# A gated linear recurrence and a gated feed-forward on one core: the order lists behind the first sums laid out anew

## The chip, the cores and the metric

The kernel runs on one core of a Trainium2 chip. Its measure is the device time of one execution in microseconds (us), lower is better. The kernel before took 194.64 us, the median of three runs (194.61, 194.64, 195.2).

## What is computed

Two operations follow each other. The first is a recurrence over 768 time steps for 4 batches of 8 heads with 48 dimensions, the second a feed-forward over the 3072 rows that come out of it.

```python
def _attn_ref(q, k, v, f_logit):
    f = 1.0 / (1.0 + np.exp(-f_logit))
    state = np.zeros((B, H, D, D))
    for t in range(S):
        state = f[:, :, t, :, None] * state + np.einsum('bhd,bhe->bhde', k[:, :, t], v[:, :, t])
        y[:, :, t] = np.einsum('bhd,bhde->bhe', q[:, :, t], state)
    return y

x = attn_out.transpose(0, 2, 1, 3).reshape(B * S, H * D)       # 3072 x 384
gate = np.maximum(x @ w_gate, 0.0)                              # 384 x 1536
val = x @ w_val
return gate * val @ w_out                                       # 1536 x 384
```

## The kernel before, in words

Time is cut into 6 chunks of 128 steps. The work is told by (chunk c, position b), four positions to a chunk; the first eight such pieces are done two at a time as a "unit" (two chunks of one batch), the others one batch each. For every piece the kernel sums -log f along time with a matmul (`cum`), takes exponentials of the sums (`ek`, `eq`), scales k and q by them (`hk`, `hq`, the tile `hats`), transposes these (on TensorE as `tk`, `tq` with copies `ck`, `cq` into `qkT` for the first eight pieces, with a DMA, `xh`, for the others), forms scores (`s`), masks them (`m`, into `ptm`), and multiplies by v (`y`, and `yi` for what comes from the state). `kv` is the chunk's contribution to the state, `ss`, `sd` and `st` (VectorE or GpSimd) bring the state forward. The result goes, transposed, into `xT` (`x`, or `n` and a DMA `xx`).

The feed-forward of a chunk has 12 slices of 128 hidden columns: a gate group `g` and a value group `u` (three matmuls each), relu `r`, product `p` into `gT`, and then per position three output groups `o` of four matmuls, a copy `d` and a store `S`. In chunk 0 the first four slices are done in two halves of 256 columns (`g00.j`, `g02.j`), the others over 512.

An operation's name is the short name with chunk and position: `hk10` is k scaled for chunk 1, position 0; `g00.8` is gate slice 8 of chunk 0; `o03.4` the second output group of chunk 0, position 3. Loads of inputs are named `f1.2`, `k1.0` and so on (384 KB each, for two positions); those of the weights `wg4+4` (gate slices 4 to 7), `wv0+2`, `wo8+4`. Weights are converted to bf16 by the transfer and are issued by GpSimd's queue (POOL), inputs by SP and ScalarE (ACT), stores by SP.

The program decides no order by itself. Each operation is an `Op` with a number, with one or more engines that can do it, and with what it reads and writes. `Plan.link` (line 127) derives the dependences. The lists in `ORDER` (line 23) give for every engine the numbers in the order of issue, and by standing in a list an operation is put on that engine. `BANKS` gives each accumulator its PSUM bank, in the order of TensorE's list. A negative entry `~3512` in TensorE's list means three filler matmuls of 512 columns on zeros (line 877); ahead of them TensorE already waits for whatever holds the next operation's bank. `HELD` adds waits by hand: `51: 53` makes operation 51 (`wg0+2`) wait until 53 (`k0.2`) has landed; as lists are issued in order, what stands behind 51 in its queue waits too. `Plan.waits` (line 187) turns dependences into semaphore waits.

Numbers that come up: 66 `q1.2`, 59 `k1.0`, 60 `q1.0`, 65 `k1.2`, 64 `f1.2`, 61 `v1.0`, 67 `v1.2`, 70 `wo0+2`, 52 `wv0+2`, 51 `wg0+2`, 57 `wv2+2`, 62 `wg4+4`, 63 `wv4+4`, 69 `wv8+4`, 68 `wg8+4`, 71 to 73 the other `wo`; 117 and 127 `hq02`, `hq03`; 116 and 126 `hk02`, `hk03`; 236 and 246 `hk10`, `hk11`; 273 `hq12`; 102 `y00`; 266 `ef12` (exponential of f, line 478); 159 `r00.3`; 150 `g00.1`; 289 `s12`; 302 `g10.0`; 806 `q5.2`; 928 and 929 the copy and store of the last piece's 256 columns, 933 and 934 of its 128.

Of the kernel before, what the change touches and what calls it, by code (L numbers as in the profile page):

```python
# [21 lines left out]

ORDER = {
    "PE": [
        45, ~60100, 76, 87, ~4512, 84, ~3512, 92, 82, 103, ~2512, 94, ~1512, 112, 123, 97, ~2512, 120, ~2512, 130, ~3512,
        118, ~3512, 102, 106, 139, 128, ~3512, 158, 133, 232, 154, 243, 150, 152, ~1512, 146, 156, 160, 138, 142, 268, 279,
# [13 lines left out]
    ],  # L40
    "ACT": [
# [8 lines left out]
    ],  # L50
    "DVE": [
# [12 lines left out]
    ],  # L64
    "POOL": [
# [4 lines left out]
    ],  # L70
# [5 lines left out]
    ],  # L76
}

HELD = {
    51: 53, 59: 62, 61: 71, 63: 58, 65: 63, 66: 57, 70: 55, 71: 60,  # L80
}

BANKS = [
# [9 lines left out]
]  # L93


# [847 lines left out]
```

## Time and profile before

| what | value |
|---|---|
| median of the runs | 194.64 us |
| the profiled execution | 195.66 us, span 193.8 us |
| TensorE (PE) busy | 187.2 us, 97% |
| of it fillers of 512 columns | 24 matmuls; 60 more of 100 columns ahead of the first data |
| VectorE (DVE) busy | 141.4 us, 73% |
| ScalarE (ACT) / GpSimd (POOL) busy | 89.1 us / 53.1 us |
| transfers | 32.44 MB, 110311 packets |
| first filler-free stretch, `g00.0` | starts at 23.48 us |
| chunk 1's first gate group, `g10.0` | starts at 55.39 us |

The profiled execution is 1.0 us longer than the median of the runs; times within the profile are counted from the start of the span. A row of the timeline gives start, duration, engine, line and operation, out<-in, the number of instructions, and in brackets the idle time before it with what ended it. In the queues' rows stand packets, MB and the time that the packets took as a share of 16 engines; q0 is the queue of the weights, q1 SP's, q10 ScalarE's.

### The profile page before, as it was taken

What the parts mean: (1) busy time and instruction counts of PE and PEld (TensorE: products, weight loads), DVE (VectorE), ACT (ScalarE), POOL (GpSimd) and SP (SyncE); (2) the same over time, 40 slices, a digit from 0 to 9 for tenths busy, and PEclk for the clock granted to TensorE, in tenths of its full rate; (3) what the DMA queues carried; (4) which work ended last, traced back from release to release, by engine and by line L of the source; (5) the groups of instructions that cost most, each with busy time, mean ns of one, the idle gap of its engine ahead of it and who ended that gap; (6) DMA issues with size and microseconds to landing.
All of it is one profiled execution on the core that took longest, in us unless ns stands there. A gap on an engine that the chain in (4) does not pass through costs nothing.

```text
span 193.8 us, 4881 instructions
## 1 busy us (share of the span) xinstructions
PE 187.2 (97%) x2009; PEld 109.5 (57%) x2009; DVE 141.4 (73%) x264; ACT 89.1 (46%) x191; POOL 53.1 (27%) x84
## 2 busy tenths in 40 slices
PE   7899999999899999999999999999999999999994
PEld 7555676565554555655546755656555565555554
DVE  4486957896946899988998878988649585373331
ACT  2776962340189931274624895663241313424300
POOL 8867500920338204134011415227100000000000
PEclk9999999999999999999999999999999999999999
DMA  5999999999998999999999988757670022002113
GB/s 148 325 284 211 139 192 260 215 195 263 244 221 176 251 199 192 192 239 190 255 215 184 218 238 171 155 145 148 139 191 3 20 81 64 16 26 81 41 43 123
DMA packets 110311, 32.44 MB, mean 167 GB/s; under 512 B 103504, under 2 KB 110032, under 8 KB 110288
## 3 DMA queue, kind: packets, MB, share of 16 engines
q1 hardware_dynamic: 93056, 25.04, 58.5%
q0 software_dynamic: 3776, 3.54, 11.6%
q10 hardware_dynamic: 13456, 3.54, 8.2%
q8 instruction: 16, 0.26, 0.5%
q14 instruction: 7, 0.06, 0.1%
HBM read 25.95 MB, written 4.72 MB: 158 GB/s over the span
## 4 chain that ended last, share of the span: by engine, by line
PE 70%; DMA 19%; ACT 4%; POOL 4%; issue 1%; ACTq 0%; DVE 0%; POOLq 0%; DVEq 0%
PE ps L792 39%; PE ps L813 20%; DMA k_in<-in_k_dram 9%; DMA v_in<-in_v_dram 5%; DMA wg<-in_moe_w_gate_dram 3%; POOL hats L540 3%; DMA wo<-in_moe_w_out_dram 2%; PE ps L584 2%; PE ps L503 1%; PE ps L745 1%; PE ps L772 1%; ACT expo L516 1%; PE ps L756 1%; ACT bneg L481 1%; ACT expo L518 1%
## 5 line engine op out<-in xcount | busy, mean ns | idle before, releaser
L800 DVE TENSOR_TENSOR gT<-relu,ps 128x512 bf16<-128x512 bf16 (+1 forms) x76 | 48.6, 655 | 22.1 <-PE ps L792 16.2
L792 PE MATMUL ps<-xT,wv 128*128 128x512 bf16 (+1 forms) x228 | 58.0, 368 | 0.2 <-issue 0.2
L792 PE MATMUL ps<-xT,wg 128*128 128x512 bf16 (+1 forms) x228 | 57.8, 368 | 0.2 <-ACT xT L597 0.2
L813 PE MATMUL ps<-wo,gT 128*128 128x384 bf16 (+2 forms) x300 | 51.9, 320 | 0.3 <-DMA wo<-in_moe_w_out_dram 0.3
L797 ACT ACTIVATE relu<-ps 128x512 bf16<-128x512 f32 (+1 forms) x47 | 27.2, 584 | 39.8 <-PE ps L792 19.8
L813 PEld LDWEIGHTS ps<-wo,gT 128*128 128x128 bf16 x300 | 27.6, 98 | 19.0 <-DMA wo<-in_moe_w_out_dram 0.7
L792 PEld LDWEIGHTS ps<-xT,wv 128*128 128x128 bf16 x228 | 23.3, 108 | 19.6 <-issue 0.7
L792 PEld LDWEIGHTS ps<-xT,wg 128*128 128x128 bf16 x228 | 23.4, 108 | 19.0 <-ACT xT L597 1.0
L592 DVE TENSOR_TENSOR ptm<-ps,tri 128x512 bf16<-128x512 f32 x32 | 20.2, 682 | 3.5 <-PE ps L584 3.5
L798 DVE TENSOR_SCALAR relu<-ps 128x512 bf16<-128x512 f32 (+1 forms) x29 | 18.3, 639 | 3.9 <-PE ps L792 3.5
L819 ACT ACTIVATE osb<-ps 128x384 f32<-128x384 f32 (+1 forms) x13 | 6.3, 485 | 31.4 <-PE ps L813 21.3
L540 POOL TENSOR_TENSOR hats<-k_in,expo 128x384 bf16<-128x384 f32 x15 | 14.9, 998 | 21.3 <-ACT expo L516 20.8
L540 POOL TENSOR_TENSOR hats<-q_in,expo 128x384 bf16<-128x384 f32 x10 | 10.9, 1097 | 18.1 <-DMA q_in<-in_q_dram 11.9
L518 ACT ACTIVATE expo<-ps 128x384 f32<-128x384 f32 x24 | 11.5, 494 | 6.2 <-PE ps L503 2.4
L516 ACT ACTIVATE expo<-ps 128x384 f32<-128x384 f32 x24 | 11.5, 493 | 4.8 <-POOL hats L540 2.9
L478 ACT ACTIVATE f_in<-f_in 128x768 f32<-128x768 f32 x12 | 10.1, 844 | 5.5 <-DMA f_in<-in_f_logit_dram 5.4
L456 POOL TENSOR_TENSOR st<-ssum,dec 128x384 bf16<-128x384 f32 x7 | 6.1, 865 | 22.2 <-DVE ssum L454 22.2
L877 PE MATMUL ps<-zeros 128*128 128x100 bf16 (+1 forms) x84 | 11.9, 310 | 0.1
L570 POOL CAST vpad<-v_in 128x384 bf16<-128x384 f32 x12 | 6.5, 560 | 19.9 <-DMA v_in<-in_v_dram 15.6
L820 DVE COPY osb<-ps 128x384 f32<-128x384 f32 (+1 forms) x12 | 6.4, 533 | 7.0 <-PE ps L813 6.8
L541 DVE TENSOR_TENSOR hats<-q_in,expo 128x384 bf16<-128x384 f32 x14 | 9.5, 696 | 1.6 <-ACT expo L518 1.6
L657 DVE TENSOR_TENSOR ptm<-ps,tmask 128x512 bf16<-128x512 f32 x16 | 10.1, 683 | 0.3 <-PE ps L650 0.3
(78 smaller groups left out, 171.6 us busy)
## 6 DMA issues: line engine op xcount, KB each, us to landing
out_dram<-osb SPq DMA_DIRECT2D x23, 192.0 KB, 2.2
f_in<-in_f_logit_dram SPq DMA_DIRECT2D x11, 384.0 KB, 6.6
k_in<-in_k_dram SPq DMA_DIRECT2D x11, 384.0 KB, 6.0
q_in<-in_q_dram SPq DMA_DIRECT2D x10, 384.0 KB, 6.1
v_in<-in_v_dram SPq DMA_DIRECT2D x7, 384.0 KB, 5.8
v_in<-in_v_dram ACTq DMA_DIRECT2D x5, 384.0 KB, 6.8
q_in<-in_q_dram ACTq DMA_DIRECT2D x2, 384.0 KB, 10.4
wg<-in_moe_w_gate_dram POOLq DMA_DIRECT2D x2, 384.0 KB, 9.5
```

Of the source, the lines that this page charges most:

```text
L478: add(f"ef{c}{b0}", by("ACT", lambda: sc.activation(raw, raw, AF.Exp, scale=-1.0), act_(n)), keys, keys, key=P)
L516: add(f"ek{c}{b}", by("ACT", lambda: sc.activation(ex[:, 1, :], bc.ap[:, 0:HD], AF.Exp, scale=1.0), act_(HD)), [bc], [f"expk{ei}"], key=P + 1)
L518: add(f"eq{c}{b}", by("ACT", lambda: sc.activation(ex[:, 0, :], bc.ap[:, 0:HD], AF.Exp, scale=-1.0), act_(HD)), [bc], [f"expq{ei}"], key=P ...
L540: return {**by("POOL", lambda: gp.tensor_tensor(o, i_, e_, ALU.mult), pool_(HD)), **by("DVE", lambda: ve.tensor_tensor(o, i_, e_, ALU.mult ...
L592: add(f"m{c}{b}{j}", by("DVE", lambda b=b, j=j, mi=mi: ve.tensor_tensor(ptm[mi][:, j, :, :], s[b, j].ap[:, :].rearrange("p (n t) -> p n t" ...
L657: add(f"m{c}{b2[i]}{j}", by("DVE", lambda i=i, j=j, mask=mask: ve.tensor_tensor(ptm[mi[i]][:, j, :, :], s[j, i].ap[:, :].rearrange("p (n t ...
L792: z = te.matmul(bank.ap[:, 0:n], wt[:, kt, w_cols(j)], xT[xi][:, kt, n0:n1], start=(kt == 0), stop=(kt == NK - 1))
L797: add(f"r{c}{b0}.{j}", {**by("ACT", lambda: sc.activation(rdst, gate.ap[:, 0:n], AF.Relu), act_(n)), **by("DVE", lambda: ve.tensor_scalar_ ...
L798: **by("DVE", lambda: ve.tensor_scalar_max(rdst, gate.ap[:, 0:n], 0.0), dve_(n))}, [gate], [f"relu{ri}"], key=P)
L800: add(f"p{c}{b0}.{j}", by("DVE", lambda: ve.tensor_tensor(gT[gi][:, j, n0:n1], rdst, val.ap[:, 0:n], ALU.mult), dve_(n)), [val, f"relu{ri} ...
L813: z = te.matmul(o.ap[:, 0:e1 - e0], gT[gi][:, j, b * C:(b + 1) * C], wo[:, j, e0:e1], start=(j == 0), stop=(j == NJ - 1))
L877: te.matmul((op.opens[0].ap if op.opens else banks[7])[:, 0:fill % 1000], zeros[:, 0:128], zeros[:, 0:fill % 1000], start=True, stop=True, ...
```

## The change

The lists of all five engines, the banks and the holds are replaced from behind the first sums (`cum00`, `cum01` and the transposes that follow) to the end. No operation is added or removed and none computes anything else; 104 of the 935 stand on another engine, the fillers are 25 of 512 columns instead of 24. In a few words it is described as: all orders and holds behind the first sums laid out anew, with weight slices counted as beginning later behind their issue. That counting was done where the lists were made; in the kernel only its outcome stands.

The core of the diff (the lists go on in the same manner):

```diff
     "PE": [
-        45, ~60100, 76, 87, ~4512, 84, ~3512, 92, 82, 103, ~2512, 94, ~1512, 112, 123, 97, ~2512, 120, ~2512, 130, ~3512,
-        118, ~3512, 102, 106, 139, 128, ~3512, 158, 133, 232, 154, 243, 150, 152, ~1512, 146, 156, 160, 138, 142, 268, 279,
...
+        45, ~60100, 76, 87, ~4512, 84, ~3512, 92, 82, 103, ~2512, 94, 123, 112, 97, ~7512, 120, ~2512, 130, 102, 128, 106,
+        118, 139, 158, 133, 154, 232, 243, ~7512, 150, 152, 146, 138, 279, 268, 142, 156, 160, 148, 174, 176, 170, 172, 186,
+        166, 168, 182, 162, 164, 178, 180, 188, 184, 190, 192, 276, 202, 198, 194, 204, 240, 206, 250, 200, 284, 208, 274,
+        196, 248, 238, 286, 220, 289, 225, 226, 221, 210, 211, 253, 212, 227, 294, 295, 222, 215, 298, 259, 216, 258, 262,
...
-        916, 912, 917, 920, 921, 922, 925, 926, 927, 930, 931, 932,
+        922, 930, 931, 932, 926, 927,
     "ACT": [
-        49, 47, 54, 74, 75, 78, 79, 88, 89, 77, 110, 93, 111, 114, 115, 124, 125, 122, 113, 131, 119, 105, 230, 109, 231,
-        159, 266, 233, 234, 245, 244, 235, 267, 141, 145, 270, 271, 269, 167, 163, 187, 191, 280, 207, 249, 281, 199, 251,
-        285, 61, 67, 802, 377, 213, 297, 265, 301, 378, 218, 379, 315, 389, 390, 307, 391, 382, 383, 411, 381, 412, 420, 339,
+        49, 47, 54, 74, 75, 78, 79, 88, 89, 77, 110, 93, 111, 124, 132, 114, 125, 115, 113, 131, 105, 230, 231, 266, 159,
+        233, 245, 235, 234, 155, 244, 267, 147, 141, 269, 270, 271, 175, 171, 187, 167, 183, 179, 191, 280, 277, 199, 281,
+        285, 275, 67, 61, 370, 373, 297, 223, 301, 265, 378, 218, 379, 303, 391, 389, 390, 381, 383, 382, 307, 228, 411, 412,
...
     "DVE": [
-        95, 108, 132, 117, 99, 127, 121, 100, 98, 101, 140, 129, 143, 144, 136, 135, 134, 155, 151, 137, 153, 147, 157, 161,
+        95, 100, 101, 98, 99, 121, 126, 116, 129, 109, 119, 140, 143, 137, 144, 136, 134, 135, 151, 153, 145, 157, 161, 149,
+        177, 173, 169, 163, 165, 181, 189, 185, 236, 246, 193, 203, 237, 195, 247, 241, 282, 251, 272, 201, 205, 283, 197,
+        239, 287, 249, 207, 209, 292, 293, 290, 291, 288, 257, 256, 213, 255, 252, 296, 242, 254, 260, 263, 261, 299, 315,
...
     "POOL": [
-        25, 1, 36, 37, 38, 2, 4, 34, 11, 5, 20, 13, 7, 14, 8, 33, 26, 3, 39, 35, 16, 41, 17, 56, 40, 90, 91, 70, 52, 116, 51,
-        126, 57, 62, 63, 69, 68, 273, 236, 246, 71, 72, 73, 395, 387, 242, 288, 278, 264, 300, 392, 428, 385, 393, 410, 425,
+        25, 1, 36, 37, 38, 2, 4, 34, 11, 5, 20, 13, 7, 14, 8, 33, 26, 3, 39, 35, 16, 41, 17, 56, 40, 90, 91, 70, 52, 108,
+        122, 117, 127, 51, 57, 62, 63, 69, 68, 273, 71, 72, 73, 278, 264, 428, 420, 300, 392, 384, 395, 405, 393, 425, 418,
...
     "SP": [
-        46, 48, 50, 55, 53, 58, 64, 66, 59, 60, 65, 373, 371, 370, 374, 372, 214, 219, 376, 512, 375, 229, 386, 394, 224,
+        46, 48, 50, 55, 53, 58, 64, 66, 59, 60, 65, 517, 377, 376, 371, 214, 519, 374, 219, 372, 375, 512, 229, 515, 394,
...
 HELD = {
-    51: 53, 59: 62, 61: 71, 63: 58, 65: 63, 66: 57, 70: 55, 71: 60,
+    51: 53, 57: 58, 59: 63, 63: 58, 65: 69, 67: 71, 70: 50, 71: 60, 72: 54, 517: 68,
 }
```

78 rows, old and new, of tables (BANKS, ORDER) are left out of this document.

## The prediction

> **What bounds the kernel now.** I read the page's first two parts first, to see which engine is the limit, then TensorE's timeline, to see where it still waits, then the DMA queues by stretch, because three of those waits end with a transfer.
>
> ```profile
> PE 187.2 (97%) x2009; PEld 109.5 (57%) x2009; DVE 141.4 (73%) x264; ACT 89.1 (46%) x191; POOL 53.1 (27%) x84
> ...
> PEclk9999999999999999999999999999999999999999
> DMA  5999999999998999999999988757670022002113
> ```
>
> TensorE (PE) is busy 97% of the span at full granted clock, and the transfers are at nine tenths until slice 27. So time can be won only by taking out fillers (matmuls on zeros, line 877) or waits of PE. Groups of 3 x 512 columns start 0.647 us apart when nothing waits, four of 384 columns 0.65, a filler 0.22. These are the places where PE waits after 33 us:
>
> ```profile
> 33.94 0.81 PE L792 MATMUL ps<-xT,wv 128*128 128x512 bf16 x3
> 35.20 0.38 PE L552 MATMUL ps<-ident,hats 128*128 128x128 bf16 x4 [0.45 <-POOL hats L540]
> ...
> 45.12 1.14 PE L813 MATMUL ps<-wo,gT 128*128 128x384 bf16 x6
> 46.52 0.34 PE L813 MATMUL ps<-wo,gT 128*128 128x384 bf16 x1 [0.27 <-DMA wo<-in_moe_w_out_dram]
> ...
> 51.34 0.82 PE L813 MATMUL ps<-wo,gT 128*128 128x384 bf16 x4
> 52.51 0.52 PE L695 MATMUL ps<-vpad,hats 64*128 64x96 bf16 x16 [0.35 <-POOL vpad L570]
> ```
>
> Counted start to start they cost 35.20-33.94-0.65 = 0.61 (tq12 waits for hq12, and that for the load q1.2, landed 33.92), 46.52-45.12-6x0.163 = 0.43 (slice wo8+4) and 52.51-51.34-0.65 = 0.52 (v12, behind load v1.2): 1.56 us.
>
> From g10.0, the first feed-forward group of chunk 1, at 55.39 to PE's end at 191.4 lie 136.0 us, of which the groups' own spacings are 135.1. There is almost nothing left to win behind 55 us.
>
> The transfers, in packets by queue (q0: the weights, issued by POOL; q1: SP's loads), for 13.2 to 15.7, 24 to 26 and 28 to 30 us:
>
> ```profile
> q1 hardware_dynamic: 2075, 0.79, 114.8%
> ...
> q0 software_dynamic: 334, 0.33, 108.1%
> ...
> q0 software_dynamic: 292, 0.28, 83.9%
> q1 hardware_dynamic: 295, 0.11, 32.5%
> ```
>
> Slice wo0+2 was issued at 12.57 and had moved nothing by 15.7; load q1.2, issued at 22.67, had moved nothing by 26. So a load begins some 3 to 4 us behind its issue when the other queue is full, and then both queues take turns, packet by packet (292 to 295). A unit load has 64 packets on each of the 16 engines, a weight slice 24 (wo0+2: 8). Alone, q1 moves 2075/2.5/16 = 52 a us and engine.
>
> **The change part by part.**
>
> *PE's own work* is the same but for one filler more (84 before, 85 now): +0.22 us, all of it ahead of 22.5 us.
>
> *Up to g00.1.* Nothing changes before 11.3 us. POOL's wo0+2 now waits for f0.2 (landed 10.19) instead of v0.2 (12.27): it issues at 11.35 and wv0+2 at 11.95 to 12.7. Then POOL takes sd10 (0.83), v02 (0.5), hq02 and hq03, which were DVE's or ACT's. ACT: PE does cum03 first, done 12.80; ek03 12.84, v03 13.22, eq02 13.63 to 14.12, eq03 to 14.5, dc02, ek02 to 15.2 (0.38 apart, dc 0.36). POOL's hq02 is then 14.2 to 15.2 and hq03 to 16.1 (0.95 apart). DVE, freed of both, does the four masks of s00 at once, 13.95 to 16.46 (0.60 apart). PE: y00 at 16.5 (17.56 before); hk03 and hk02, now on DVE, end 17.3 and 17.7; x01 ends 18.66, so g00.3 starts 18.7 (20.18 before). ss11 ends 20.0 (cum10), m031 20.6 (cum11 to 20.95). Seven fillers (1.54) then stand ahead of g00.1: 22.5 against 22.37 before. The early gain goes into fillers. ACT's ef12 and r00.3 stand ahead of those fillers: ef12 is due at 19.3 and needs load f1.2.
>
> *From g00.1 to g10.0* the same groups are done in both orders: 14 half-width gate and value groups at 0.327 (4.58), 16 full ones at 0.647 (10.35), 12 output groups at 0.65 (7.80), eight transposes (1.78), three y at 0.667, three yi at 0.273, two s at 0.573, two kv at 0.446, cum12 and cum13 (0.86): 30.2 us (before 0.22 more, a filler). Before took 55.39-22.37 = 33.0, so 2.6 of waits: the 1.56 above, 0.6 of waits under 0.25, some 0.4 of 0.09 us steps where a small group follows a large one. What becomes of them:
> - tq12: q1.2 is no longer held for wv2+2 (before issued 22.67), it follows f1.2 at 12.6 and rides between weight packets; landed by about 28, needed at 34. 0.61 goes. It is costed on weights that don't move much: wg0+2 and wv2+2 issue 0.3 and 1.2 us earlier. wg8+4, wanted at 34.3, landed 33.74; cover is thin here (0.5 us).
> - wo8+4: POOL no longer stands in hk10 and hk11 when q1.0 lands (those two, 1.0 us each, were ahead of wo2+2's issue at 37.03, and go to DVE). Issued about 35, the three land about 2 us earlier; wanted at 46.8 against 44.5: 0.43 goes.
> - v12: ACT now issues v1.2 ahead of v1.0, at about 40.5 (before 42.09), landing about 47 to 48.5 (v1.0 took 6.8 from 41.69) for y12 at 48.1. 0.52 goes.
> - New: DVE has 12 instructions between g00.8 and s12 (r00.8 to cq13: four of 512 columns at 0.60, four hats at 0.47, four q/k copies at 0.33 to 0.37), with the latencies at both ends 5.95 us, and PE gives it 5.45: +0.5. kv12 waits for d00, which DVE reaches behind v13, m111, m110: +0.25. x11 on ACT ends 0.15 behind g10.0's turn.
>
> So waits of 0.9, and 0.4 of steps: g10.0 at 22.5+30.2+1.3 = 54.0 against 55.39, -1.35. I add 0.1 for f1.2, below: -1.25.
>
> *Behind g10.0* PE's work is 135.1 us in both. I summed each stretch of DVE, ACT and POOL between a PE result and the PE group that needs it, against PE's spacings: before has one of 0.46 too much (d22 to ln42, where the trace shows 0.29), the changed order none over 0.05. DVE has 2 us more over the run, ACT 5 less, POOL 6 more. Nothing is taken for it. Cover: loads f2.2, q2.0, k2.2, f3.0 now stand behind S00 and v3.2 in SP's queue (before v3.2 was issued at 82); I place q2.0 at about 61 (57.96 before) for hq20 at 62. ACT issues q5.2 among its expo work near 67 us; the first such issue in an empty queue took 0.37 (84.31), a second one right behind 3.30 (85.41).
>
> *The end.* The last pieces are swapped. Before, the 64 KB store came last: DVE's copy 0.29, landing 1.53. Now the 128 KB one: ACT's copy 0.38, landing 1.71: +0.27.
>
> Sum on the profiled span: 193.8-1.25+0.27 = 192.8, that is -1.0; the same difference on the median of the runs (194.64; the profiled execution took 195.66 with 1.9 us outside its span) gives **193.7 us**.
>
> **The rivals.**
>
> *f1.2 comes late (slower).* wo0+2 and wv0+2 issue 1.2 us earlier, into the middle of f1.2. With wo0+2's 3.2 us from issue to first packet they start at 14.5, when the slowest engine has some 80 packets of f1.0 and f1.2 to go. 32 pass in turns (8 at 0.15, 24 at 0.07: 3 us), then 50 are left at 17.4. If wg0+2, issued 16.2, starts only at 18.4, they pass alone and f1.2 lands at 18.5; if weights follow without a gap, at 21.8. ef12 holds r00.3, that the fillers, that g00.1: each us behind 19.3 is a us of PE, and none of it comes back, since later loads land before they are needed. 21.8 gives +2.3: 195.9. For it: f1.2 landed at 18.07 with wo0+2 1.2 us later. Against it: a gap of over 1 us in q0 is what the trace shows behind wg2+2 as well. [...]
>
> *k1.0 holds DVE (same or slower).* k1.0 now waits for wv4+4 (27.88 before) instead of wg4+4 (25.76), and hk10, hk11 moved to DVE, where p00.7, r00.10, hq10 and the 12 instructions above are queued behind them. Before, k1.0 took 9.28 from issue. I place it at 33 to 34, since q1 has no q1.2 ahead of it and weights end by then. From 34.3 on every us costs PE one at tq10 (DVE needs 2.75 from its landing to hq10; PE is there at 37.1). Landing at 35.06 as before: +0.75, 194.4. At 28+9.3 = 37.3: +3.0, 196.7.
>
> *A load of chunk 2 late, or ACT held in an issue.* q2.0 at 64 instead of 61 stops DVE for 2 us at hq20, with PE some 1 us behind: 194.7. q5.2 blocked as at 85.41: +2.3 through ln30 to cum30, 196.0.
>
> *The waits only change places*: 194.6. Each wait named new above is of the size of one removed.
>
> **How the numbers follow.** Forecast 0.45 (192.7 to 194.0), f1.2 late 0.2, k1.0 late 0.18, chunk 2 or the issue 0.1, places changed 0.07. A difference of 0.3% (0.58 us) is about what can be told from none: faster is below 194.06, slower above 195.22. Faster: the forecast's 0.45 and a part of the mild ends, 0.46. Same: mild f1.2 and k1.0, and places changed, 0.19. Slower: 0.35. The range leaves out the upper tenth and little below: 192.7 to 196.1.
>
> **What would show it.** In the changed profile: y00's group (line 672) near 16.5; the first 128x256 value group near 22.8; tq12 without a wait; g10.0 (line 792 behind the last output group of chunk 0) near 54.1; a wait of about 0.5 ahead of the second s group (line 650) near 42. ACT idle ahead of f_in at 19 to 22 us shows the first rival, DVE idle ahead of hats<-k_in at 33 to 37 the second. The prediction is wrong if g10.0 stands behind 55 us, or if PE's work from there takes over 137.

## The result and the profile after

The changed kernel takes 193.87 us, the median of 22 runs (193.69 to 195.15), against 195.16 for the kernel before on the same chips (22 runs, 194.61 to 196.29): ratio 0.9933, 95% interval 0.992 to 0.9947. It is 1.3 us faster. The forecast was 193.7. The base moved too: the 194.64 from which it was counted is at the low end of the kernel before's runs, so the gain is 0.3 us larger than the 1.0 forecast and the base 0.5 higher. All medians here and below leave out three runs of the kernel of experiment 4 that took 197.8 to 198.1 us at a granted clock of 0.991.

The page's first two parts for the changed kernel (those of before stand in the prediction):

```profile
PE 185.4 (97%) x1992; PEld 110.1 (57%) x2010; DVE 146.3 (76%) x264; ACT 83.3 (43%) x183; POOL 59.8 (31%) x92
...
DMA  5999999999989997999989997991337010000413
```

TensorE is the bound as before (granted clock 1.0). Its weight loads (PEld) number 2010, but only 1992 matmuls are recorded: 18 records are missing, so the start of a group is read from its weight load where needed. The transfers stay near nine tenths up to slice 27.

TensorE's timeline of the changed kernel (start, duration, engine, line, operation, count, and in brackets the idle time ahead):

```profile
16.45 0.74 PE L672 MATMUL ps<-ptm,vpad 64*32 64x128 bf16 x64
...
22.82 0.49 PE L792 MATMUL ps<-xT,wv 128*128 128x256 bf16 x3
...
33.60 0.81 PE L792 MATMUL ps<-xT,wv 128*128 128x512 bf16 x3
34.25 0.39 PE L552 MATMUL ps<-ident,hats 128*128 128x128 bf16 x4
...
41.33 0.81 PE L813 MATMUL ps<-wo,gT 128*128 128x384 bf16 x4
42.35 0.64 PE L650 MATMUL ps<-qkT 48*64 48x128 bf16 x32 [0.21 <-DVE qkT L556]
...
53.99 0.76 PEld L792 LDWEIGHTS ps<-xT,wg 128*128 128x128 bf16 x5 [0.35 <-ACT xT L597]
...
124.98 0.81 PE L792 MATMUL ps<-xT,wv 128*128 128x512 bf16 x3
126.01 0.82 PE L813 MATMUL ps<-wo,gT 128*128 128x384 bf16 x4 [0.22 <-DVE gT L800]
```

y00 stands at 16.45, the first value group at 22.82, tq12 follows its predecessor at the spacing of an unhindered group (34.25-33.60 = 0.65), a wait of 42.35-41.33-0.65 = 0.37 stands ahead of s12, and g10.0 starts at 54.0. Near 126 there is a wait that before did not have: o33.0 stands 0.39 late behind product p30.1 on DVE.

Start to start, by these rows and those of before:

| stretch | before | after | difference |
|---|---|---|---|
| to g00.1 | 22.37 | 22.49 | +0.12 |
| g00.1 to g10.0 | 33.02 | 31.52 | -1.50 |
| g10.0 to PE's end | 135.99 | 135.30 | -0.69 |
| PE's end to the span's end | 2.42 | 2.69 | +0.27 |
| span | 193.8 | 192.0 | -1.80 |

The profiled execution of before is 0.5 us over the median of its runs, which accounts for 1.8 here against 1.3 in the medians.

Where the load q1.2 went, as the issues of two stretches (before, 22 to 24 us; after, 12 to 14 us), the last column is the time to landing in us:

```profile
q_in<-in_q_dram SPq DMA_DIRECT2D x1, 384.0 KB, 11.3
```

```profile
q_in<-in_q_dram SPq DMA_DIRECT2D x1, 384.0 KB, 8.8
```

It lands at 21.1 in place of 33.9, and what stands behind it in SP's queue comes sooner too: k1.0 at 31.9 (35.1) and q1.0 at 33.1 (36.3). So do slice wo8+4, at 42.1 (46.5), which stands behind wo2+2, held for q1.0, and v1.2, at 45.9 (51.4), which in the kernel before could only follow wo2+2's landing.

### The profile page after: what moved, and what is told of

Read it like the earlier page. It is cut to its first block, busy times and chain, and to the rows that moved or that the text cites. A ratio compares the mean times of both kernels' runs of the same rounds, so it can differ in the third digit from the quotient of the medians.

```text
span 192.0 us, 4872 instructions
## 1 busy us (share of the span) xinstructions
PE 185.4 (97%) x1992; PEld 110.1 (57%) x2010; DVE 146.3 (76%) x264; ACT 83.3 (43%) x183; POOL 59.8 (31%) x92
## 4 chain that ended last, share of the span: by engine, by line
PE 83%; DVE 5%; DMA 4%; ACT 3%; issue 1%; POOL 1%; SPq 1%; ACTq 0%
PE ps L792 43%; PE ps L813 25%; DMA f_in<-in_f_logit_dram 4%; PE ps L584 2%; DVE gT L800 2%; PE ps L745 2%; DVE hats L541 2%; PE ps L672 1%; PE ps L503 1%; PE ps L494 1%; POOL hats L540 1%; PE ps L772 1%; PE ps L650 1%; PE ps L756 1%; DVE qkT L556 1%
## 5 line engine op out<-in xcount | busy, mean ns | idle before, releaser
L792 PE MATMUL ps<-xT,wv 128*128 128x512 bf16 (+1 forms) x225 | 57.0, 368 | 0.3
L792 PE MATMUL ps<-xT,wg 128*128 128x512 bf16 (+1 forms) x216 | 55.2, 367 | 0.7 <-issue 0.2
L797 ACT ACTIVATE relu<-ps 128x512 bf16<-128x512 f32 (+1 forms) x39 | 21.8, 565 | 48.5 <-PE ps L792 27.5
L798 DVE TENSOR_SCALAR relu<-ps 128x512 bf16<-128x512 f32 (+1 forms) x37 | 24.9, 674 | 5.8 <-PE ps L792 4.8
L570 POOL CAST vpad<-v_in 128x384 bf16<-128x384 f32 x14 | 7.5, 549 | 43.7 <-PE ps L745 22.6
L540 POOL TENSOR_TENSOR hats<-q_in,expo 128x384 bf16<-128x384 f32 x14 | 14.5, 1044 | 9.6 <-ACT expo L518 9.1
L540 POOL TENSOR_TENSOR hats<-k_in,expo 128x384 bf16<-128x384 f32 x13 | 13.8, 1071 | 6.5 <-ACT expo L516 3.7
L456 POOL TENSOR_TENSOR st<-ssum,dec 128x384 bf16<-128x384 f32 x11 | 9.7, 878 | 17.1 <-DVE ssum L454 17.0
L597 ACT ACTIVATE xT<-ps 128x384 bf16<-128x384 f32 x10 | 5.4, 549 | 17.9 <-PE ps L672 8.6
L481 ACT ACTIVATE bneg<-f_in 128x768 bf16<-128x768 f32 x12 | 10.1, 842 | 0.2
## 6 DMA issues: line engine op xcount, KB each, us to landing
out_dram<-osb SPq DMA_DIRECT2D x23, 192.0 KB, 2.8
```

Of the source, the lines that this page charges most:

```text
L540: return {**by("POOL", lambda: gp.tensor_tensor(o, i_, e_, ALU.mult), pool_(HD)), **by("DVE", lambda: ve.tensor_tensor(o, i_, e_, ALU.mult ...
L792: z = te.matmul(bank.ap[:, 0:n], wt[:, kt, w_cols(j)], xT[xi][:, kt, n0:n1], start=(kt == 0), stop=(kt == NK - 1))
L797: add(f"r{c}{b0}.{j}", {**by("ACT", lambda: sc.activation(rdst, gate.ap[:, 0:n], AF.Relu), act_(n)), **by("DVE", lambda: ve.tensor_scalar_ ...
L798: **by("DVE", lambda: ve.tensor_scalar_max(rdst, gate.ap[:, 0:n], 0.0), dve_(n))}, [gate], [f"relu{ri}"], key=P)
```

## The experiments

Medians are of several runs each; beside them the kernel before ran on the same chip (195.1 to 195.4). Offsets "against the changed kernel" are to 193.87, which was measured beside a before of 195.16. The ratios' intervals of the changed kernel and of runs 5, 6 and 8 overlap, so their differences of 0.3 us are not settled by these medians alone; for runs 5 and 6 the timelines carry the reading, for run 8 the pair of kernels in run 10, which ran on one chip.

**1. The hold on q1.2 put back.**

```diff
-    51: 53, 57: 58, 59: 63, 63: 58, 65: 69, 67: 71, 70: 50, 71: 60, 72: 54, 517: 68,
+    51: 53, 57: 58, 59: 63, 63: 58, 65: 69, 67: 71, 70: 50, 71: 60, 72: 54, 517: 68, 66: 57,
```

> The changed kernel with load q1.2 held back until slice wv2+2 has landed, as in before: issue near 22.9 in place of 12.3. Theory A (the prediction's step: the hold made tq12's wait): q1.2 lands about 11 us behind its issue as before, near 34, hq12 ends near 35.2, tq12 waits about 0.9 at 34.25, and k1.0, behind it in the same queue, comes to hk10 1 to 2 us late: 1 to 2 us slower than the changed kernel. Rival (the weights' earlier end, 30.7 in place of 33.7, would have done it alone): q1.2 lands at 31 to 33, hq12 ends by 34, no wait at tq12 over 0.2, and since wg0+2 no longer shares the engines with q1.2 it lands near 20.7 in place of 22.0; the time is the changed kernel's within 0.3 us.

Measured: 194.52 us, ratio to before 0.9955 (0.9935 to 0.9975). q1.2 issued at 22.1 and landed at 33.99; k1.0 landed at 34.97, wo8+4 at 45.4, v1.2 at 48.3, all 2.4 to 3.2 us later. TensorE's timeline of this run:

```profile
33.85 0.81 PE L792 MATMUL ps<-xT,wv 128*128 128x512 bf16 x3
35.27 0.38 PE L552 MATMUL ps<-ident,hats 128*128 128x128 bf16 x4 [0.60 <-POOL hats L540]
```

tq12 waits 35.27-33.85-0.65 = 0.77, kv12 another 0.4 (for d00, on DVE behind the cast of the late v1.2), and g10.0 stands at 55.4: in this profile 1.4 us of the gain ahead of g10.0 are gone, in the medians 0.65. Theory A's mechanism holds; its size, 1 to 2 us, was too large by the medians (0.65).

**2. The hold taken out of the kernel before, nothing else.**

```diff
-    51: 53, 59: 62, 61: 71, 63: 58, 65: 63, 66: 57, 70: 55, 71: 60,
+    51: 53, 59: 62, 61: 71, 63: 58, 65: 63, 70: 55, 71: 60,
```

> One part of the change alone: the kernel before without the hold on load q1.2, which then issues near 12.3 behind f1.2, and nothing else changed. Theory A (from the run with q1.2 held: this hold cost tq12's wait and made every later load land about 3 us later): q1.2 lands near 21, k1.0 near 32 to 33, tq12's wait of 0.61 goes, the waits at o00.4 (slice wo8+4) and kv12 (load v1.2) shrink with the earlier loads, wg0+2 lands near 22 and costs up to 0.2 at g00.1: g10.0 at 53.9 to 54.7 in place of 55.4, the time 0.7 to 1.4 us under before. Rival (the new order of the engines is what takes the waits out, and in the old order the load's time only moves them): g10.0 at 55.0 to 55.4, time within 0.3 us of before.

Measured: 193.81 us, ratio 0.9915 (0.9884 to 0.9947). One number out of the lists gives as much as the whole change.

```profile
33.83 0.81 PE L792 MATMUL ps<-xT,wv 128*128 128x512 bf16 x3
34.48 0.39 PE L552 MATMUL ps<-ident,hats 128*128 128x128 bf16 x4
```

tq12 no longer waits, the 0.43 ahead of o03.8 is gone (wo8+4 landed 43.6 in place of 46.5), kv12's 0.52 is 0.27, and g10.0 stands at 53.85. Theory A.

**3. The change in two halves.** All engines follow the changed order up to chunk 0's last output group (with the loads that it has begun by then), then that of before; and the other way round. Banks were renumbered at the joint.

> All orders are the changed kernel's up to the last output group of chunk 0 (loads started by then with them); behind it every engine goes on in the order of before, the end too. Theory A (the gain has two places, 1.38 us ahead of g10.0 and 0.69 behind it, less 0.27 at the end): g10.0 at 54.0 as in the changed kernel, PE from there 136.0 as before, with the waits of 0.34 at g10.1 and 0.29 at kv41 back: PE ends at 190.0, 1.4 us sooner than before, span 192.4. Theory B (the prediction as it stood: all of the gain is ahead of g10.0, and what is saved behind it is a chance of the one profiled execution): PE from g10.0 takes about 135.3 here too, and the time is at or below the changed kernel's, -1.7 to -2.0 us against before. Theory C (the loads of chunk 2 that the changed order starts early are needed for its gain): a wait of 1 us or more between 58 and 75 us, and a time less than 0.7 us under before.

> The other half: the orders of before up to the last output group of chunk 0, then the changed kernel's, its end with them. Theory A: g10.0 at 55.4 as before, PE from there 135.3 (before 136.0), the tail 0.27 longer: 0.4 us sooner than before. Theory B: g10.0 at 55.4, PE from there 136.0, tail 0.27 longer: 0.3 us slower than before. In both the wait of 0.39 ahead of o33.0 (near 127) should be there if it is DVE's order that makes it.

Measured: 194.68 (0.998, 0.9959 to 1.0002) for the changed front alone, 196.27 (1.0045, 1.0024 to 1.0067) for the changed back alone: -0.6 and +1.0 against before, where the whole gives -1.3. So A falls, and B too. In the first, g10.0 stood at 54.3 but a wait of 0.74 came at kv22 (69.84): hk22 stands far back in DVE's row there. In the second, TensorE stood still for 0.78 at 58 (a pause of another kind, see run 7), 0.35 ahead of s22 (transpose xh22 late in SP's queue, landed 79.57) and 0.55 ahead of cum32 (ACT waited 3.75 for load f3.2, until 83.67). Apart from the 0.78, this fits halves that were each laid out for the loads that the other one starts, but no run tests that reading. C is nearest, with a wait of 0.74 for the 1 that it named.

**4. Two moves undone together:** hk10 and hk11 back to POOL ahead of wo2+2's issue, v1.0 ahead of v1.2 on ACT.

```diff
 POOL:
-     ... 69, 68, 273, 71, 72, 73,
+     ... 69, 68, 273, 236, 246, 71, 72, 73,
 ACT:
-     285, 275, 67, 61, 370,
+     285, 275, 61, 67, 370,
```

> The changed kernel with two of its moves undone: hk10 and hk11 are POOL's again and stand ahead of the issue of wo2+2, and ACT issues v1.0 ahead of v1.2. The prediction gave the first 0.43 (slice wo8+4) and the second 0.52 (v12). Theory A (the loads of chunk 1, 3 us earlier by q1.2's early issue, have taken both waits out already): hk10 and hk11 end near 34 on POOL, the slices issue 0.7 later and wo8+4 lands near 43 against 46.8; v1.2 lands near 47.4 and v12 ends near 48.0 against 48.3; no new wait over 0.2 and the changed kernel's time within 0.3 us. Rival (the prediction's steps): a wait of 0.2 to 0.5 ahead of o00.8 or y12 comes back, and the time is 0.4 to 0.9 us over the changed kernel's.

Measured: 194.84 (0.9991, 0.996 to 1.0022), 1.0 us over the changed kernel. wo8+4 landed at 43.1 and nothing waited for it: the first move is worth nothing here. v1.2 landed at 47.8 in place of 45.9, and that is not covered. DVE's timeline, then TensorE's:

```profile
47.87 0.36 DVE L571 CAST vpad<-v_in 128x384 bf16<-128x384 f32 x1 [1.52 <-DMA v_in<-in_v_dram]
```

```profile
48.88 0.73 PE L672 MATMUL ps<-ptm,vpad 64*32 64x128 bf16 x64 [0.54 <-DVE ptm L657]
49.95 0.51 PE L695 MATMUL ps<-vpad,hats 64*128 64x96 bf16 x16 [0.33 <-DVE osb L820]
```

v13's cast stands in DVE's row ahead of m111, m110 and d00, so a late v1.2 stops the row: y12 waits 0.70 for m111, kv12 0.40 for d00. The rival held for this move, in the new order: a wait came back and the time rose.

**5. One copy from DVE to ACT** (ck10, number 239, to ACT ahead of f2.0's issue).

```diff
 DVE:
-     ... 283, 197, 239, 287, 249,
+     ... 283, 197, 287, 249,
 ACT:
-     285, 275, 67, 61, 370,
+     285, 275, 67, 61, 239, 370,
```

> The changed kernel with one copy, ck10 (out of PSUM, 0.41 us), moved from DVE to ACT, where it stands ahead of the issue of f2.0. Theory A (the prediction's step: s12 waits for DVE's row of twelve that ends with cq13): cq13 ends 0.34 sooner, the wait of 0.38 ahead of s12 near 41.9 shrinks to 0.05 and g10.0 comes at 53.7; 0.3 us of the time go. Rival 1 (the row behind it on DVE, d00 to x10, is what sets g10.0): s12 comes sooner but g10.0 stays at 54.0. Rival 2 (f2.0 and v2.0 issue 0.4 later and hold ACT longer, x12, x13 or x11 come late): g10.0 at 54.2 or later.

Measured: 193.60 (0.9904, 0.9875 to 0.9934), 0.27 under the changed kernel. TensorE's timeline:

```profile
41.53 0.81 PE L813 MATMUL ps<-wo,gT 128*128 128x384 bf16 x4
42.28 0.64 PE L650 MATMUL ps<-qkT 48*64 48x128 bf16 x32
```

42.28-41.53-0.65 = 0.10 where 0.37 stood, and g10.0 came 31.2 behind g00.1 in place of 31.5. Theory A: DVE's row of twelve set s12.

**6. The last two pieces in the order of before.**

```diff
-        922, 930, 931, 932, 926, 927,
+        922, 926, 927, 930, 931, 932,
 SP:
-     ... 919, 924, 934, 929,
+     ... 919, 924, 929, 934,
```

> The changed kernel with the last two pieces of the output in the order of before: the 128 KB piece first, the 64 KB piece last. Theory A (the prediction's step): DVE's copy of 0.29 and a landing of 1.5 stand last in place of ACT's 0.38 and 1.7, so the span from PE's last matmul to the end is 2.4 us in place of 2.7: span 191.7, 0.27 us sooner than the changed kernel. Rival: the last store waits for the first one's packets or for the issue of SP, and the end stays where it is, within 0.1 us.

Measured: 193.61 (0.9912, 0.9888 to 0.9936), 0.26 under the changed kernel; PE's end 189.35, span 191.8: 2.4 us behind PE in place of 2.7. Theory A.

**7. Fewer fillers ahead of g00.1.**

```diff
-     ... 232, 243, ~7512, 150,
+     ... 232, 243, ~1512, 150,
```

> The changed kernel with one filler in place of seven ahead of g00.1: 1.3 us less of PE's own work. Theory A (the fillers only cover the landing of slice wg0+2, 22.04): g00.1 starts at 22.1 to 22.2 in place of 22.5, PE waits there for the slice, g10.0 at 53.7, and 0.3 us of the time go. Rival 1 (behind g00.1 something else is late by as much, cum13's ln12 with its 0.43 or x03 with its 0.28): g10.0 stays at 54.0, time unchanged within 0.15. Rival 2 (without fillers the granted clock falls or the slice's wait costs more than the fillers): slower by 0.3 us or more, the clock below full somewhere behind 21 us.

Measured: 194.72 (0.9974, 0.9954 to 0.9994), 0.85 slower than the changed kernel, and none of the three foresaw why. g00.1 started at 22.08, and PE kept the lead until 50.4. Then, in the middle of the group yi13 (twelve matmuls), with its only wait long past:

```profile
50.37 0.29 PE L708 MATMUL ps<-qkT,st 128*32 128x128 bf16 x7
51.85 0.27 PE L708 MATMUL ps<-qkT,st 128*32 128x128 bf16 x5 [1.19 <-issue]
```

"issue" is a wait for nothing that the profile shows; the granted clock was 1.0. Two more rows of this kind, from the changed back alone and from the kernel before:

```profile
57.30 0.81 PE L792 MATMUL ps<-xT,wv 128*128 128x512 bf16 x3
58.72 0.34 PE L503 MATMUL ps<-bneg,tri 128*128 128x384 bf16 x1 [0.62 <-issue]
```

```profile
57.60 0.81 PE L792 MATMUL ps<-xT,wg 128*128 128x512 bf16 x3
58.58 0.82 PE L792 MATMUL ps<-xT,wv 128*128 128x512 bf16 x3 [0.18 <-issue]
```

Counting TensorE's instructions from the program's start (a weight load and a matmul each, and waits that stand alone), the last two pauses stand at the same number, 1730, though in different groups, and the first one at 1474, which is 256 less. The page has a queue for instructions (packets, MB, share; here of the changed kernel):

```profile
q8 instruction: 16, 0.26, 0.6%
```

These are 16 transfers of 16 KB, and TensorE has some 4070 instructions: one for every 256. Set side by side (times in us):

| kernel | PE passes | transfer behind it | 256 instructions on |
|---|---|---|---|
| changed | 1218 at 46.3 | 46.7 to 48.0 | no pause |
| one filler | 1218 at 45.9 | 49.1 to 50.4 | pause of 1.4 until 51.85 |
| before | 1474 at 52.5 | 56.0 to 57.4 | pause of 0.34 until 58.58 |
| changed back alone | 1474 at 52.2 | 56.0 to 57.3 | pause of 0.78 until 58.72 |

Two explanations remained: the time at which PE passes the border, or the place of the border, since six instruction pairs fewer move it by six matmuls. Runs 8 and 9 part them.

**8. Short fillers:** the seven kept, but 60 columns wide (`~7060` for `~7512`), so that the count stays and the time shrinks.

> The changed kernel with the seven fillers ahead of g00.1 cut from 512 columns to 60: as many instructions as in the changed kernel, but about 1.2 us shorter, so that PE waits for slice wg0+2 as in the run with one filler (g00.1 at 22.1). There PE stood still for 1.4 us behind the eighth matmul of yi13, in the middle of a group, with nothing awaited, at its instruction 1474; a 16 KB transfer on the instruction queue had begun 3.2 us behind PE's instruction 1218 (0.4 in the changed kernel) and ended 1.4 us ahead of PE's going on. Theory A (the transfer's start depends on what the data queues hold when PE passes that instruction, so the time decides, not the number of instructions): the transfer behind instruction 1218 begins 2.5 us or more late here too, a pause of 1 us or more at instruction 1474, g10.0 near 55, the time 0.7 to 0.9 us over the changed kernel. Theory B (the six instructions fewer, which put the border of the block at another matmul, made the pause): no pause, g10.0 at 53.6 to 53.8, the time 0.2 to 0.4 us under the changed kernel.

Measured: 193.57 (0.9928, 0.9907 to 0.9948), 0.30 under the changed kernel, no pause. In the profiled execution slice wg0+2 landed at 22.75 (22.04 in the changed kernel's), so that one shows no gain, and PE passed 1218 at 46.6, no sooner than in the changed kernel. The absence of the pause fits theory B; what parts it from A is the second kernel of run 10, with the same fillers, which passed 1218 at 45.6, had its transfer from 46.2 and no pause.

**9. The same six fillers taken out where PE waits anyway,** ahead of tq02 (`~1512` for the first `~7512`).

> The changed kernel with one filler in place of the first seven ahead of tq02 (13.7 us), where PE has to wait for hq02 until 15.25 anyway: six instructions fewer, as in the run with one filler ahead of g00.1, but nothing earlier behind 15.3 us. Theory B (the border of PE's instruction block, moved by six matmuls, makes the pause): PE stands still for 1 us or more behind the eighth matmul of yi13, at its instruction 1474, and the time is 0.7 to 1.1 us over the changed kernel. Theory A (what counts is when PE passes instruction 1218 against the data queues): passed near 46.2 as in the changed kernel, so the transfer begins within 1 us, no pause, and the time is the changed kernel's within 0.2 us. A third way, not about instructions: PE idle ahead of tq02 costs clock, seen as a granted clock below 1 behind 15 us.

Measured: 194.88 (0.9978, 0.9959 to 0.9996), 1.0 over the changed kernel:

```profile
50.87 0.29 PE L708 MATMUL ps<-qkT,st 128*32 128x128 bf16 x7
52.34 0.27 PE L708 MATMUL ps<-qkT,st 128*32 128x128 bf16 x5 [1.18 <-issue]
```

The pause is back at instruction 1474, with PE passing 1218 at 46.4, as in the changed kernel; the transfer ran from 49.6 to 50.9, and the granted clock stayed at 1.0. Theory B is borne out: the place of the border decides, not the time. That the late transfer is what stops TensorE is read from the place and the times of four pauses; no run moved a transfer by itself. Why the transfer begins 3.2 us late with the border there stays open.

**10. Three repairs, and the same with short fillers.** Runs 5 and 6 together with hq51 (number 821, 1.24 us on DVE) moved behind p30.5, because p30.1, for which o33.0 waited 0.39, stood behind it:

```diff
-     ... 724, 821, 605, 593, 619, 621, 609, 683,
+     ... 724, 605, 593, 619, 621, 609, 821, 683,
```

> The changed kernel with three small repairs: the last two pieces of the output in the order of before, ck10's copy on ACT, and on DVE hq51 (1.24 us) moved from ahead of p30.4 to behind p30.5, because in the changed kernel p30.1 ends behind it and the group o33.0 waits 0.39 for it near 126. Theory A (each wait is paid where it stands and nothing near behind it is late): tail 2.4 in place of 2.7, s12's wait 0.05 in place of 0.38, no wait at o33.0, span 191.0 to 191.3, time 192.9 to 193.2, 0.7 to 1.0 us under the changed kernel. Rival 1 (the waits only move: r30.8 or p30.8 come late for s40 or o30.0, or g10.0 is set by x11): span 191.5 to 191.8. Rival 2 (PE's stream of instructions: the pause without a wait seen in the run with one filler, 1.4 us at PE's instruction 1474, comes back when PE is earlier): a gap of 0.3 or more between two matmuls of one group between 46 and 60 us.

> The three repairs and the short fillers together. Theory A of the short fillers' run: a pause of 1 us or more at PE's instruction 1474, the time 0.7 us or more over that of the three repairs alone. Theory B: no pause, 0.2 to 0.4 us under the three repairs alone, 192.5 to 192.9.

Measured: 192.87 (0.9892, 0.9874 to 0.991) and 192.56 (0.9878, 0.9859 to 0.9897). Both beat the changed kernel, by 1.0 and 1.3 us. TensorE's timeline of the second, where the two waits stood:

```profile
40.94 0.81 PE L813 MATMUL ps<-wo,gT 128*128 128x384 bf16 x4
41.68 0.64 PE L650 MATMUL ps<-qkT 48*64 48x128 bf16 x32
...
124.36 0.81 PE L792 MATMUL ps<-xT,wv 128*128 128x512 bf16 x3
125.01 0.81 PE L813 MATMUL ps<-wo,gT 128*128 128x384 bf16 x4
```

s12 comes 0.74 behind its predecessor, o33.0 0.65, g00.1 starts at 22.10 and no pause follows. The first run came out at theory A (192.9 to 193.2 named), the second at theory B.

## Why the prediction was right, and where it was not

That 193.7 lies 0.2 us from 193.87 is in part luck: the kernel before was 0.5 slower than the base of the forecast, and the gain 0.3 larger than forecast, mostly in a stretch for which nothing was taken.

*Up to g00.1*: right. y00 16.45 (16.5 forecast), g00.3 18.60 (18.7), g00.1 22.49 (22.5). The early gain did go into fillers; short ones give 0.3 of it back (193.57; 192.56 against 192.87), and no more is to be had there while wg0+2 lands at 22.0 or later.

*f1.2* landed at 19.78 against 19.3 due. ef12 ended at 20.64, r00.3 at 20.92, and the fillers began at 20.98: cum11 ahead of them, started at 20.55, would have let them begin at about 20.87, so the late load cost about 0.1, the allowance made for it. The first rival did not come, and its rule that each us behind 19.3 is a us of PE was too strict by some 0.4 us of cover. Its mild end, which the chances count as "same", stands in no run: f1.2 cost that 0.1. *k1.0* landed at 31.9, before the 33 to 34 of the sum, and hk10 waited for nothing; the second rival did not come either. q2.0 landed at 60.4 (61), q5.2's issue on ACT took 0.37 at 65.4: nothing of the third.

*g00.1 to g10.0*: the sum was right (54.0 to 54.1; measured 54.0), its causes only in part. tq12's 0.61 went with the hold, as said. But the 0.43 at wo8+4 was put down to POOL being free of hk10 and hk11, and the 0.52 at v12 to the exchange of v1.2 and v1.0. Run 2 shows that the first and half of the second go with the hold alone, since every later load comes about 3 us sooner; the step looked at q1.2's own user and not at the queue behind it. Run 4 shows the first move to be worth nothing, while the exchange is needed in the new order. Of the new waits, s12's 0.5 measured 0.37 and x11's 0.15 measured 0.15; kv12's 0.25 did not come, d00 ended 0.20 ahead of its turn.

*Behind g10.0* lies the failed step: "Nothing is taken for it". It kept all of the 0.9 us of waits that before has there and allowed for none that are new. Measured: 135.30 in place of 135.99, -0.69. The two largest, 0.34 behind g10.1 and 0.29 behind kv41 (where ln42 is late), are gone, with 0.17 ahead of cum33 and some five steps of 0.1 where a small group follows a large one; a new wait, 0.39 at o33.0, is there, which the sums of engine work between groups ("none over 0.05") missed. The 0.29 in the kernel before (114.58-114.12-0.17):

```profile
114.12 0.33 PE L772 MATMUL ps<-vpad,hats 128*128 128x96 bf16 x4
114.58 0.34 PE L503 MATMUL ps<-bneg,tri 128*128 128x384 bf16 x1
```

That the old order costs this much is no accident of one profile: run 2, with the old order, took 135.89 (kv41's 0.29 is there again, the 0.34 is not, and 0.24 stands ahead of kv22), and the new order took 135.29 to 135.32 in eight kernels. The 0.34 was no wait of the program at all but a pause that goes with a late transfer of instructions (run 7).

The new wait shows a cost that the sum lacked. DVE's hq51, ahead of p30.1, took 1.24 us while GpSimd was at work; moved behind p30.5 in run 10, with GpSimd idle, the same instruction took 0.55. The changed kernel, then the second kernel of run 10 (whose GpSimd row in this stretch ends at 124.51):

```profile
123.52 1.24 DVE L541 TENSOR_TENSOR hats<-q_in,expo 128x384 bf16<-128x384 f32 x1
121.11 3.23 POOL L540 TENSOR_TENSOR hats<-k_in,expo 128x384 bf16<-128x384 f32 x3
124.30 1.14 POOL L456 TENSOR_TENSOR st<-ssum,dec 128x384 bf16<-128x384 f32 x1
```

```profile
126.44 0.55 DVE L541 TENSOR_TENSOR hats<-q_in,expo 128x384 bf16<-128x384 f32 x1
123.68 0.83 POOL L456 TENSOR_TENSOR st<-ssum,dec 128x384 bf16<-128x384 f32 x1
```

In all the traces of this case, 153 such scalings on DVE with GpSimd idle took 0.54 to 0.56 us, and 56 that ran beside more than 0.8 us of GpSimd's work took 1.07 to 1.37; the others lie between. The 0.69 that hq51 took longer is more than the wait of 0.39, so, as an estimate, p30.1 would have been in time without it; no run has hq51 in its place with GpSimd idle. DVE's work as a whole grew by 4.9 us (146.3 against 141.4), not by the 2 of the sum.

*The end*: +0.27 forecast, +0.27 in the trace, 0.26 in run 6.

*The rival that the waits only change places* was nearer than its 0.07: against the kernel before without its one hold (193.81), the whole new layout (193.87) brings nothing that can be seen.

## What to carry to other kernels

Before an order is laid out anew, take out each wait written by hand on its own: here one held load made the loads behind it in its queue, and what waited for them, land 2.4 to 3.2 us later (run 1), and that one hold was worth the whole change (run 2). When a wait is to be priced, list every later load of that queue and its user, and count the waits that stand in the far stretches as part of the change, on both sides. Price an instruction of DVE by what runs on GpSimd beside it (hq51: 1.24 us with GpSimd at work, 0.55 with it idle). When TensorE stops inside a group with nothing awaited, count instructions: six matmuls fewer far ahead made such a pause (1.19 and 1.18 us without a matmul) in runs 7 and 9.

## What the hardware showed that was not expected

TensorE's instructions, by these counts, come in blocks of 256 by 16 KB transfers of 0.9 to 1.6 us each, on a queue that the page lists among those of the data: the changed kernel has 16 such borders and 16 transfers, each begun between 2.8 us ahead of its border and 3.2 us behind it. Between 46 and 58 us, where TensorE does 256 instructions in 4.5 to 5.9 us (many matmuls of 96 and 128 columns), a transfer begun within 1.9 us of the border cost nothing; begun 3.2 to 3.8 us late it went with a pause of TensorE of 0.34 to 1.4 us, which ended 1.2 to 1.5 us behind the transfer's end (in run 2, 3.2 us late, only 0.08 was lost). Elsewhere such a delay cost nothing: near 14, 20 and 27 us the transfers begin 1.7 to 3.7 us late in every kernel, and near 38 us one of the kernel before began 6.0 us late; there 256 instructions take 5.9 to 15 us. Each of the four pauses stands one block of 256 instructions behind the border whose transfer was late (1474 behind 1218, 1730 behind 1474); why it stands there is not shown here.

DVE's scaling of q or k (128x384 out of f32) takes 0.55 us with GpSimd idle and 1.07 to 1.37 beside more than 0.8 us of GpSimd's work (the counts above). Why is not shown here.
